# Transposed keys copied by ScalarE, six value buffers, and the sums for the output products one to a gap

## The chip, the core and the metric

The kernel runs on one core of a Trainium2 chip. The metric is the device time of one execution in microseconds. With each execution comes the core's span (about 2 us shorter: 335.8 of 337.71 us in the profile of before) and the mean clock that TensorE was granted over it, 1.0 being full speed.

## The reference

Attention over pooled keys and values, then a gated feed-forward layer, on 8 batches of 576 tokens with 8 heads of 64.

```python
k_p = k.reshape(B, H, Sp, 8, D).mean(axis=3)          # 72 pooled keys and values per head
v_p = v.reshape(B, H, Sp, 8, D).mean(axis=3)
attn = softmax(q @ k_p.T / 8)                          # cut: maximum and epsilon
x = (attn @ v_p) -> [4608 tokens, 512]
out = (np.maximum(x @ w_gate, 0.0) * (x @ w_val)) @ w_out      # 512 -> 1536 -> 512
```

## The kernel before

It is software-pipelined by hand. A loop turns over chunks of 512 tokens. Turn c runs twelve gate units of chunk c (eight 512-column matmuls each, then a relu on ScalarE and a multiplication on VectorE), the seven output products of chunk c - 1 in a scheme of the Strassen kind that needs four sums S of parts of h, and the attention of batch c + 1 (scores, exponential, value pieces with their division). GpSimd pools the keys and values of later batches meanwhile.

```python
piece_pool = ctx.enter_context(tc.tile_pool(name="piecep", bufs=4))
ps_at = ctx.enter_context(tc.tile_pool(name="ps_at", bufs=3, space=bass.MemoryType.PSUM))
...
def k_transposes(b):                       # keys of batch b, transposed in PSUM, copied out
    ps = ps_mm.tile([P, KJ + 1, KROWS], F16, name="mm_ps", tag="mm_ps")
    k_windows(b, ps, 0, KJ + 1)
    k_evacuate(b, ps, False, nc.vector)
    k_evacuate(b, ps, True, nc.vector)
...
def values(b, t):                          # one value piece: two halves, a PSUM buffer each
    x = piece_pool.tile([P, NG, 2, D], F16, name="px")
    rd = piece_pool.tile([P, 2, NG // 2, 2], F32, name="prd")
    for half in range(2):
        ps = ps_at.tile([P, 512], F32, name="at_ps", tag="at_ps")
        ...                                # four matmuls
        nc.vector.reciprocal(out=rd[:n, half], in_=pv[:, :, D:D + 2])
        nc.vector.tensor_tensor(out=x[...], in0=pv..., in1=rd..., op=ALU.mult)
...
for c in range(1, n_chunks):               # the turns
    ...
    prods, sums = out_products(c - 1)      # sums: S0 to S3, each in two halves
    ...
    others, later = attention(c + 1)       # [[keys], [], score trios ..., value pieces ...]
    for i, piece in enumerate(left):       # two pieces of batch 2, left over from turn 1
        others[1 + i].insert(0, piece)
    ...
    for i, unit in enumerate(units):
        unit()                             # a gate unit or a product
        ...
        elif i:
            run(sums[2 * i - 2:2 * i])     # two halves to a gap
        ...
        run(others[i])
```

The softmax here doesn't subtract the row's maximum and nothing guards it: scores larger than these inputs give would overflow.

Of the kernel before, what the change touches and what calls it, by code (L numbers as in the profile page):

```python
# [16 lines left out]
def kernel(  # L17
# [10 lines left out]
    nc = tc.nc  # L28

    B, H, S, D = q.shape  # L30
# [10 lines left out]
    n_chunks = NTOK // TCH  # L41
# [25 lines left out]
    relu_pool = ctx.enter_context(tc.tile_pool(name="relup", bufs=3))  # L67
    fout_pool = ctx.enter_context(tc.tile_pool(name="foutp", bufs=2))
    pexp_pool = ctx.enter_context(tc.tile_pool(name="pexpp", bufs=2))
    piece_pool = ctx.enter_context(tc.tile_pool(name="piecep", bufs=4))  # L70
    ps_mm = ctx.enter_context(tc.tile_pool(name="ps_mm", bufs=4, space=bass.MemoryType.PSUM))
    ps_at = ctx.enter_context(tc.tile_pool(name="ps_at", bufs=3, space=bass.MemoryType.PSUM))
    ps_acc = ctx.enter_context(tc.tile_pool(name="ps_acc", bufs=1, space=bass.MemoryType.PSUM))
# [43 lines left out]
    def as_rows(src, b):  # L117
        return src[b].rearrange("h (s t) d -> s h (t d)", t=POOL)
# [4 lines left out]
    def load_k(b):  # L123
        tl = kin_pool.tile([P, KJ, POOL, D], F16, name="k_in")
        k_tiles[b] = tl
        flat = k[b].rearrange("h (p j t) d -> (h p) j (t d)", p=KP, t=POOL)
        nc.gpsimd.dma_start(out=tl[:KROWS].rearrange("p j t d -> p j (t d)"), in_=flat)

    def load_v(b):
        tl = vin_pool.tile([P, H, POOL, D], F16, name="v_in")  # L130
        v_tiles[b] = tl
        nc.gpsimd.dma_start(
            out=tl[:SP].rearrange("s h t d -> s h (t d)"), in_=as_rows(v, b))
# [28 lines left out]
    def load_q(b, i0=0, n=NI):  # L162
        if b not in q16_tiles:
            q16_tiles[b] = q16_pool.tile([P, QT * D], F16, name="q16")
        cols = slice(i0 * 2 * D, (i0 + n) * 2 * D)
        flat = q[b].rearrange("h (p t) d -> (h p) (t d)", p=QP)
        nc.gpsimd.dma_start(out=q16_tiles[b][:, cols], in_=flat[:, cols])
# [22 lines left out]
    def pool_k(b, i, eng):  # L190
        src = k_tiles[b][:KROWS, 2 * i:2 * i + 2].rearrange("p j t d -> p j (t d)")
        return tree(eng, KROWS, src,
                    kps[b % 2][:KROWS, 1 + 2 * i:3 + 2 * i, :])

    def pool_v(b, g, eng):
        st = stats[b % 2][:SP, g, :].rearrange("p (x d) -> p x d", d=D)[:, 0::3, :]
        src = v_tiles[b][:SP, 2 * g:2 * g + 2].rearrange("p h t d -> p h (t d)")
        return tree(eng, SP, src, st)
# [38 lines left out]
    def run(pieces):  # L237
        for piece in pieces:
            piece()
# [7 lines left out]
    def k_windows(b, ps, w0, n):  # L247


        for w in range(w0, w0 + n):  # L250
            nc.tensor.transpose(
                out=ps[:, w, :],
                in_=kps[b % 2][:KROWS, w:w + 2, :].rearrange("p j d -> p (j d)"),
                identity=ident16[:KROWS, :KROWS])

    def k_evacuate(b, ps, upper, eng):

        ds, x, w = (slice(D, P), 1, 0) if upper else (slice(0, D), 0, 1)
        dst = kpTs[b % 2][x].rearrange("d h (s j) -> d h s j", j=KJ)[ds]
        src = ps.rearrange("d w (h s) -> d h s w", h=H)[ds, :, :, w:w + KJ]  # L260
        if eng is nc.scalar:
            eng.copy(dst, src)
        else:
            eng.tensor_copy(out=dst, in_=src)

    def k_transposes(b):
        ps = ps_mm.tile([P, KJ + 1, KROWS], F16, name="mm_ps", tag="mm_ps")
        k_windows(b, ps, 0, KJ + 1)
        k_evacuate(b, ps, False, nc.vector)
        k_evacuate(b, ps, True, nc.vector)  # L270

    qT_tiles = {}

# [14 lines left out]
    def q_dma(b):  # L288

        qT_tiles[b] = qT_pool.tile([P, NI, P], F16, name="qT")  # L290
        nc.sync.dma_start_transpose(
            out=qT_tiles[b], in_=q16_tiles[b].rearrange("p (i d) -> p i d", d=P))
# [124 lines left out]
    h_tiles = {}  # L417

    def gate_val(c, fo, t0=0, n=TCH):
        p0 = (c * TCH + t0) % RING  # L420
        cuts = [0, n] if p0 + n <= RING else [0, RING - p0, n]
        fsl = slice(fo * P, (fo + 1) * P)
        ps = []
        for w in (wg_sb, wv_sb):
            t = ps_mm.tile([P, TCH], F32, name="mm_ps", tag="mm_ps")
            for lo, hi in zip(cuts, cuts[1:]):
                x0 = (p0 + lo) % RING
                for ci in range(n_co):
                    nc.tensor.matmul(  # L429
                        out=t[:, lo:hi], lhsT=w[:, ci, fsl], rhs=x_T[:, ci, x0:x0 + hi - lo],  # L430
                        start=(ci == 0), stop=(ci == n_co - 1),
                    )
            ps.append(t)
        relu = relu_pool.tile([P, TCH], F16, name="relu")
        nc.scalar.activation(out=relu[:, :n], in_=ps[0][:, :n], func=AF.Relu)  # L435
        if c not in h_tiles:
            h_tiles[c] = h_pool.tile([P, n_fo, TCH], F16, name="h")
        nc.vector.tensor_tensor(  # L438
            out=h_tiles[c][:, fo, t0:t0 + n], in0=ps[1][:, :n], in1=relu[:, :n], op=ALU.mult)
# [48 lines left out]
    def weight_sums():  # L488

        e, f = wo_sb[:, :n_hf, :HD], wo_sb[:, :n_hf, HD:]  # L490
        g, h = wo_sb[:, n_hf:, :HD], wo_sb[:, n_hf:, HD:]
        t1, t2, t3, t4 = [wo_sums[:, i] for i in range(4)]
        return [lambda o=o, x=x, y=y, i=slice(i, i + 2): nc.vector.tensor_tensor(
                    out=o[:, i], in0=x[:, i], in1=y[:, i], op=ALU.subtract)
                for o, x, y in ((t1, f, e), (t2, h, t1), (t3, h, f), (t4, g, t2))
                for i in range(0, n_hf, 2)]
# [175 lines left out]

    gate = const_pool.tile([P, 1], F16, name="gate")

    def prep(b, load_next, behind=None):

        for i in range(KJ // 2):
            run(pool_k(b, i, nc.gpsimd))
        if behind is not None:
            nc.gpsimd.tensor_copy(out=gate, in_=behind)  # L680
        if load_next:
            load_k(b + 1)
            load_q(b + 1)
            load_v(b + 1)
        for g in range(NG):
            run(pool_v(b, g, nc.gpsimd))

# [22 lines left out]
    def weave_units(units, others):  # L710

        n, m, seq = len(others), len(units), []
        for i, unit in enumerate(units):
            seq += [unit] + others[i * n // m:(i + 1) * n // m]
        return seq

    with tc.manual_schedule():
# [110 lines left out]
             pv[0], z[10], *Sc[14:], pv[1], z[11], V[4], o[0], V[0], x[4], o[1], V[1], x[0]])  # L828
        q_dma(2)
        run([o[2], V[2], x[1], o[3], x[2], V[3], o[4]])  # L830
        prep(2, True)

        left = []
        for c in range(1, n_chunks):
            order = range(n_fo)
            if c == n_chunks - 1:

                order = [fo for i in range(n_hf) for fo in (i, n_hf + i)]
            gv = [lambda fo=fo: gate_val(c, fo) for fo in order]

            if c == 1:
                sums = weight_sums()
                units = weave_units(gv[:-1], o[5:])
            else:
                prods, sums = out_products(c - 1)
                units = []
                for fo in range(n_fo - 1):
                    units.append(gv[fo])
                    if prods and (fo not in (1, 4, 7, 10) or c == n_chunks - 1):
                        units.append(prods.pop(0))  # L850
            others = []

            prep_at = 3
            if c + 1 < B:
                others, later = attention(c + 1)
                for i, piece in enumerate(left):
                    others[1 + i].insert(0, piece)
                left = later
            if c + 2 < B:
                others[7 if c == 1 else 1].append(lambda: q_dma(c + 2))  # L860
            if c == 1:
                others[0] = [x[3]]
            for i, unit in enumerate(units):
                if i == prep_at and c + 2 < B:
                    prep(c + 2, c + 3 < B, h_tiles[c][:, 1, :1] if c > 1 else None)
                unit()
                if c == 1:
                    run(sums[i:i + 1])
                elif i:
                    run(sums[2 * i - 2:2 * i])  # L870
                if i in (0, 1) and sends:
                    sends.pop(0)()
                if i < len(others):
                    run(others[i])
                if c == n_chunks - 1:
                    if i == 14:
                        tail, last_sums = last_products(c)
                        run(last_sums[0])
                    elif i == 16:
                        run(last_sums[1])  # L880
            gv[-1]()
# [32 lines left out]
```

## Time and profile before

| | before |
|---|---|
| median of three executions | 334.46 us (334.33 to 334.75) |
| the execution that the profile shows | 337.71 us, span 335.8, mean clock 0.990 |
| TensorE busy | 325.3 us, 97% of the span |
| VectorE, ScalarE, GpSimd busy | 214.7, 128.7, 139.8 us |
| turn 2 (87.09 to 127.55 us) | 40.46 us |
| turns 3, 4, 5 | 33.79, 34.01, 33.76 us |

Read it from TensorE: it is nearly always busy, so only its holes and its clock can give anything. Both lie in turn 2.

Two readings of this trace explain words of the prediction. The trace keeps the times at which TensorE's clock changed: after its first rise it was full for 88.75 us, half for 6.83 and full for 235.52, which are 26, 2 and 69 times 3.413 us. A stretch of 3.413 us, laid end to end from the first rise, is called a clock window here. At half clock four 512-column matmuls took 1.71 us from their start to the next (96.53 to 98.24), at full clock 0.86 (90.51 to 91.37). And a "contended" sum is one made while GpSimd was at work: a pair of them took 2.31 us at 91.06, so 1.16 each, and 1.03 at 165.38 with GpSimd idle from 154.13 to 167.29.

### The profile page before, as it was taken

What the parts mean: (1) busy time and instruction counts of PE and PEld (TensorE: products, weight loads), DVE (VectorE), ACT (ScalarE), POOL (GpSimd) and SP (SyncE); (2) the same over time, 40 slices, a digit from 0 to 9 for tenths busy, and PEclk for the clock granted to TensorE, in tenths of its full rate; (3) what the DMA queues carried; (4) which work ended last, traced back from release to release, by engine and by line L of the source; (5) the groups of instructions that cost most, each with busy time, mean ns of one, the idle gap of its engine ahead of it and who ended that gap; (6) DMA issues with size and microseconds to landing.
All of it is one profiled execution on the core that took longest, in us unless ns stands there. A gap on an engine that the chain in (4) does not pass through costs nothing.

```text
span 335.8 us, 6528 instructions
## 1 busy us (share of the span) xinstructions
PE 325.3 (97%) x2526; PEld 214.2 (64%) x2526; DVE 214.7 (64%) x456; ACT 128.7 (38%) x295; POOL 139.8 (42%) x186
## 2 busy tenths in 40 slices
PE   8899999999969999999999999999999999999995
PEld 2578875455536665766898966655666556566574
DVE  7465637768666757785777667766576464464562
ACT  1544562473426224722471247124822332232231
POOL 8557419999999801993099309300000000000000
PEclk9999999999969999999999999999999999999999
DMA  7999998998559246963984462243022300300224
GB/s 112 190 204 201 200 214 159 188 153 171 106 101 185 47 90 94 205 101 74 159 158 79 81 107 58 33 64 104 1 24 56 113 5 0 98 29 3 65 75 110
DMA packets 51006, 35.41 MB, mean 105 GB/s; under 512 B 30432, under 2 KB 45024, under 8 KB 50976
## 3 DMA queue, kind: packets, MB, share of 16 engines
q0 software_dynamic: 18304, 18.88, 34.3%
q1 hardware_dynamic: 32528, 16.00, 24.0%
q8 instruction: 19, 0.31, 0.4%
q10 hardware_dynamic: 144, 0.13, 0.1%
q14 instruction: 11, 0.09, 0.1%
HBM read 37.75 MB, written 9.44 MB: 141 GB/s over the span
## 4 chain that ended last, share of the span: by engine, by line
PE 90%; DVE 5%; DMA 2%; ACT 1%; issue 1%; POOL 1%; DVEq 0%; ACTq 0%; POOLq 0%
PE mm_ps L429 54%; PE acc_ps L521 19%; PE at_ps L310 5%; PE mm_ps L467 3%; PE at_ps L388 3%; PE mm_ps L594 2%; DMA q<-in_q_dram 2%; DVE px L394 1%; DVE h L438 1%; PE mm_ps L411 1%; DVE sum L512 1%; PE mm_ps L281 1%; PE mm_ps L341 1%; PE mm_ps L365 1%; ACT pexp L370 1%
## 5 line engine op out<-in xcount | busy, mean ns | idle before, releaser
L438 DVE TENSOR_TENSOR h<-mm_ps,relu 128x512 f16<-128x512 f32 (+1 forms) x120 | 76.4, 637 | 87.6 <-PE mm_ps L429 79.8
L435 ACT ACTIVATE relu<-mm_ps 128x512 f16<-128x512 f32 (+1 forms) x120 | 66.5, 554 | 137.4 <-PE mm_ps L429 135.3
L429 PE MATMUL mm_ps<-x_T,wv_sb 128*128 128x512 f16 (+1 forms) x528 | 114.0, 342 | 0.1
L429 PE MATMUL mm_ps<-x_T,wg_sb 128*128 128x512 f16 (+1 forms) x528 | 114.0, 342 | 0.0
L429 PEld LDWEIGHTS <-wv_sb 128*128 128x128 f16 x528 | 51.7, 98 | 42.9 <-issue 1.1
L429 PEld LDWEIGHTS <-wg_sb 128*128 128x128 f16 x528 | 48.7, 98 | 28.9 <-issue 1.4
L324 ACT ACTIVATE expT<-at_ps 72x288 f16<-72x288 f32 (+2 forms) x128 | 39.1, 374 | 19.0 <-PE at_ps L310 18.9
L521 PEld LDWEIGHTS <-sum 128*128 128x128 f16 x336 | 32.1, 98 | 7.2
L394 DVE TENSOR_TENSOR px<-at_ps,prd 128x256 f16<-128x256 f32 (+1 forms) x80 | 33.8, 423 | 2.7
L181 POOL TENSOR_TENSOR tree_b<-tree_a 72x256 f32<-72x256 f32 (+1 forms) x42 | 32.0, 763 | 3.3
L521 PE MATMUL acc_ps<-wo_sums,sum 128*128 128x256 f16 x252 | 31.0, 272 | 0.0
L175 POOL TENSOR_TENSOR tree_a<-v_in 72x512 f32<-72x512 f16 x24 | 29.9, 1244 | 0.1
L521 PEld LDWEIGHTS <-h 128*128 128x128 f16 x252 | 23.9, 99 | 4.1
L175 POOL TENSOR_TENSOR tree_a<-k_in 96x512 f32<-96x512 f16 x18 | 20.7, 1149 | 11.5 <-DMA k_in<-in_k_dram 11.5
L521 PE MATMUL acc_ps<-wo_sb,h 128*128 128x256 f16 x168 | 21.1, 276 | 0.0
L529 DVE TENSOR_TENSOR rows<-acc_ps,mid 128x512 f32<-128x512 f32 x21 | 14.5, 689 | 8.8 <-PE acc_ps L521 8.8
L680 POOL COPY gate<-h 128x1 f16<-128x1 f16 x4 | 1.9, 463 | 43.4 <-DVE h L438 43.4
L512 DVE TENSOR_TENSOR sum<-h 128x768 f16<-128x768 f16 x28 | 19.8, 746 | 0.1
L388 PEld LDWEIGHTS <-expT 72*128 72x128 f16 (+1 forms) x280 | 13.0, 100 | 7.5 <-DVE px L394 1.6
L393 DVE RECIPROCAL prd<-at_ps 128x4 f32<-128x4 f32 (+1 forms) x80 | 13.7, 172 | 4.0 <-PE at_ps L388 3.9
L388 PE MATMUL at_ps<-stat,expT 72*128 72x65 f16 (+1 forms) x280 | 14.8, 194 | 1.4 <-DVE px L394 1.4
L186 POOL TENSOR_TENSOR stat<-tree_b 72x128 f16<-72x128 f32 x24 | 12.1, 506 | 1.9
(106 smaller groups left out, 300.2 us busy)
## 6 DMA issues: line engine op xcount, KB each, us to landing
out_dram<-rows SPq DMA_DIRECT2D x24, 256.0 KB
k_in<-in_k_dram POOLq DMA_DIRECT2D x7, 576.0 KB, 8.0
q<-in_q_dram POOLq DMA_DIRECT2D x7, 576.0 KB, 9.9
v_in<-in_v_dram POOLq DMA_DIRECT2D x6, 576.0 KB, 13.5
wg_sb<-in_moe_w_gate_dram POOLq DMA_DIRECT2D x6, 256.0 KB, 10.9
wv_sb<-in_moe_w_val_dram POOLq DMA_DIRECT2D x6, 256.0 KB, 10.8
wo_sb<-in_moe_w_out_dram POOLq DMA_DIRECT2D x3, 512.0 KB, 9.6
v_in<-in_v_dram POOLq DMA_DIRECT2D x2, 512.0 KB, 11.3
```

The source lines that it names most:

```text
L175: eng.tensor_tensor(out=cell["a"][:n], in0=src[:, :, :4 * D], in1=src[:, :, 4 * D:], op=ALU.add)
L181: eng.tensor_tensor(out=cell["c"][:n], in0=a[:n, :, :2 * D], in1=a[:n, :, 2 * D:], op=ALU.add)
L310: nc.tensor.matmul(out=ps[:SP, c0:c0 + cnt * QP], lhsT=kpTs[b % 2][j][:, h, :], rhs=queries(b, h, i0, cnt), start=True, stop=True,)
L324: nc.scalar.activation(out=out_ap, in_=in_ap, func=AF.Exp, scale=EXP_SCALE)
L388: nc.tensor.matmul(out=ps[:n, c0:c0 + D + 1], lhsT=weights(b, h, t), rhs=stats[b % 2][:SP, g, s0:s0 + D + 1], start=True, stop=True,)
L394: nc.vector.tensor_tensor(out=x[:n, half * NG // 2:(half + 1) * NG // 2, :, :], in0=pv.rearrange("p g (x c) -> p g x c", x=2)[:, :, :, :D] ...
L429: nc.tensor.matmul(out=t[:, lo:hi], lhsT=w[:, ci, fsl], rhs=x_T[:, ci, x0:x0 + hi - lo], start=(ci == 0), stop=(ci == n_co - 1),)
L435: nc.scalar.activation(out=relu[:, :n], in_=ps[0][:, :n], func=AF.Relu)
L438: nc.vector.tensor_tensor(out=h_tiles[c][:, fo, t0:t0 + n], in0=ps[1][:, :n], in1=relu[:, :n], op=ALU.mult)
L512: nc.vector.tensor_tensor(out=S[k][:, i], in0=x[:, i], in1=y[:, i], op=op)
L521: nc.tensor.matmul(out=ps[:, tb, :], lhsT=lhs[:, i, tb * P:(tb + 1) * P], rhs=rhs[:, i, :], start=(first and tb == 0 and i == 0), stop=(tb ...
L529: nc.vector.tensor_tensor(out=out_ap, in0=x, in1=y, op=ALU.add)
```

## The change

Its intent is to take VectorE's queue off TensorE's path at the start of a turn. Three parts are named in its title; the fourth (score trios, that is the scores in threes, of turn 2 moved one unit back, in the hunk on `left`) is not. `prep` is also split in two functions, but both are called at the same place in the same order, so nothing follows from it and that part is cut here.

```diff
-    piece_pool = ctx.enter_context(tc.tile_pool(name="piecep", bufs=4))
+    piece_pool = ctx.enter_context(tc.tile_pool(name="piecep", bufs=6))
...
-        k_evacuate(b, ps, False, nc.vector)
-        k_evacuate(b, ps, True, nc.vector)
+        k_evacuate(b, ps, False, (nc.scalar if b > 2 else nc.vector))
+        k_evacuate(b, ps, True, (nc.scalar if b > 2 else nc.vector))
...
+        SUMS_AT = [1, 2, 3, 4, 5, 6, 13, 14]
...
-                for i, piece in enumerate(left):
-                    others[1 + i].insert(0, piece)
+                if left:
+                    others[1:2] = [[piece] for piece in left]
...
-                elif i:
-                    run(sums[2 * i - 2:2 * i])
+                elif c == n_chunks - 1:
+                    run(sums[max(2 * i - 2, 0):2 * i])
+                elif i in SUMS_AT:
+                    sums[SUMS_AT.index(i)]()
```

More of the change, by code (lines that the diff above doesn't have):

```diff
@@ L673, with prep_k @@
     gate = const_pool.tile([P, 1], F16, name="gate")
-    def prep(b, load_next, behind=None):
+    def prep_k(b, load_next, behind=None):
         for i in range(KJ // 2):
@@ L684, in prep, with prep_v @@
             load_v(b + 1)
+    def prep_v(b):
         for g in range(NG):
@@ L830 @@
         run([o[2], V[2], x[1], o[3], x[2], V[3], o[4]])
-        prep(2, True)
+        prep_k(2, True)
+        prep_v(2)
+        SUMS_AT = [1, 2, 3, 4, 5, 6, 13, 14]
         left = []
@@ L851 @@
             others = []
-            prep_at = 3
+            prep_v_at = 3
             if c + 1 < B:
                 others, later = attention(c + 1)
-                for i, piece in enumerate(left):
-                    others[1 + i].insert(0, piece)
+                if left:
+                    others[1:2] = [[piece] for piece in left]
                 left = later
@@ L863 @@
             for i, unit in enumerate(units):
-                if i == prep_at and c + 2 < B:
-                    prep(c + 2, c + 3 < B, h_tiles[c][:, 1, :1] if c > 1 else None)
+                if i == 3 and c + 2 < B:
+                    prep_k(c + 2, c + 3 < B, h_tiles[c][:, 1, :1] if c > 1 else None)
+                if i == prep_v_at and c + 2 < B:
+                    prep_v(c + 2)
                 unit()
```

## The prediction

> **What bounds the kernel now.** I read the page first: its busy shares, then the slices. TensorE is busy 325.3 of 335.8 us, no other engine over 64%, and the chain that ended last is 90% TensorE. So the time is the length of TensorE's stream, plus its holes, plus any time at a lowered clock. In the slices (one digit is 8.4 us) only one place away from the two ends shows both:
>
> ```profile
> PE   8899999999969999999999999999999999999995
> ...
> DVE  7465637768666757785777667766576464464562
> ...
> PEclk9999999999969999999999999999999999999999
> ```
>
> The twelfth digit, 92 to 101 us, is a 6 in the row of TensorE and a 6 in the row of its clock. The source says what lies there: the loop turns over 512-token chunks, and its turn c = 2 begins at about 87.1 us (the transposes of batch 3's pooled keys end its first unit). I cut the busy time at the turns' starts, which the chain and TensorE's timeline give (turns 2, 3 and 5):
>
> ```profile
> 87.09:127.55 40.46, 37.79 (x268) 22.83 (x267) 27.84 (x55) 13.74 (x30) 28.05 (x36) 0.92 0.52 103
> 127.55:161.34 33.79, 33.79 (x254) 21.26 (x252) 24.04 (x47) 13.52 (x30) 19.13 (x25) 1.00 0.67 120
> ...
> 195.35:229.11 33.76, 33.76 (x252) 21.18 (x251) 23.59 (x47) 13.52 (x30) 11.03 (x13) 1.00 0.41 66
> ```
>
> Columns: window, length, then busy time of PE, PEld, DVE, ACT, POOL, then clock, DMA share, GB/s. Turns 3 and 5 take 33.8 us with TensorE never idle. Turn 2 takes 40.46. It does more work by only two value pieces of batch 2 left over from turn 1, 16 small matmuls each of which the timeline places in 0.25 to 0.26 us, so it should take 33.8 + 0.5 = 34.3. **The loss there is 40.46 - 34.3 = 6.15 us**, and no other turn has one. Two-microsecond windows show its form:
>
> ```profile
> 92.00:94.00 2.00, 0.65 (x6) 0.20 (x4) 1.93 (x5) 0.17 (x1) 1.89 (x3) 1.00 0.00 0
> 94.00:96.00 2.00, 1.03 (x7) 0.66 (x8) 1.97 (x6) 0.52 (x2) 1.84 (x3) 0.72 0.09 18
> 96.00:98.00 2.00, 1.66 (x5) 0.69 (x5) 1.73 (x5) 0.70 (x2) 2.00 (x5) 0.50 0.73 138
> 98.00:100.00 2.00, 2.00 (x7) 0.67 (x5) 0.00 (x0) 0.60 (x1) 1.91 (x3) 0.50 1.10 188
> 100.00:102.00 2.00, 2.00 (x14) 1.57 (x13) 1.74 (x3) 1.00 (x3) 1.92 (x3) 0.57 1.14 213
> ```
>
> First a hole with VectorE (third busy figure) full, then half clock. The clock was at half for 1.12 us of the second row ((1 - 0.72)/0.5 x 2), all of the next two and 1.72 of the last: 6.84 us. Matmuls of 512 columns then take twice as long, so about 5.5 us of work at half clock cost 2.7 us; the holes cost the other 3.4. The timelines of TensorE and of VectorE name the cause:
>
> ```profile
> 92.33 0.32 PE L388 MATMUL at_ps<-stat,expT 72*64 72x65 f16 x4
> 94.09 0.32 PE L388 MATMUL at_ps<-stat,expT 72*64 72x65 f16 x4 [1.45 <-DVE px L394]
> 94.64 0.31 PE L310 MATMUL at_ps<-qT,kpT1l 128*72 128x288 f16 x1 [0.23 <-DVE px L394]
> ```
> ```profile
> 89.53 0.74 DVE L264 COPY kpT1l<-mm_ps 64x576 f16<-64x576 f16 x1
> 90.28 0.76 DVE L264 COPY kpT1u<-mm_ps 64x576 f16<-64x576 f16 x1
> 91.06 2.31 DVE L512 TENSOR_TENSOR sum<-h 128x768 f16<-128x768 f16 x2
> 93.39 0.18 DVE L393 RECIPROCAL prd<-at_ps 128x4 f32<-128x4 f32 x1
> 93.61 0.42 DVE L394 TENSOR_TENSOR px<-at_ps,prd 128x256 f16<-128x256 f32 x1
> ```
>
> Three PSUM buffers of the attention pool serve the value pieces and the scores. Two pieces need four. The fourth half waits for VectorE to read the first, and VectorE has 0.74 + 0.76 us of key copies and 2.31 us of sums queued ahead of that read. Turns 3 to 7 have the same VectorE queue, but no value piece beside it, so there it stays beside TensorE's work.
>
> [...] the window that dropped it (91.47 to 94.88, counting back from the drop) was not idle: from the timeline and widths TensorE worked about 30% of it. Near 13 to 16 us, between the first transposes, a window filled to about 56% did not drop it. [...] a pair of these sums takes 2.31 us while GpSimd is in its key tree (88 to 96 us), and 1.03 at 165.38 while GpSimd is idle. [...]
>
> **The change part by part.** *Key copies to ScalarE.* Ten copies (five batches, two each) leave VectorE, 5 x 1.50 = 7.5 us. On ScalarE a 16-bit copy from PSUM took 585 ns at 512 columns and 1012 at 1024, so 0.834 ns a column and 0.64 us at 576. Two take 1.25 us, in a hole of ScalarE: before its copy of the first product it idles 1.9 us in each turn. That copy comes out at about the same time (in turn 4 at about 164.7 us, as now), and the next user of its bank is 4 us off. Worth nothing in turns 3 to 6, part of the loss in turn 2.
>
> *Sums one to a gap.* The eight additions remain. The order listing puts the first after the first product, the second after the next gate unit, and the last two around the sixth product. In turn 2 only one stands before each value piece.
>
> *The left-over pieces.* The listing also shows a move that the few words do not name: in turn 2 piece one is followed by a gate unit before piece two, and every score trio comes one unit later. TensorE has 1.73 us of other work while VectorE empties the first piece.
>
> *Six buffers.* In the trace before no division waits for a transfer, so two more are worth 0.
>
> Working turn 2 by hand with the trace's durations: VectorE ends its product at 89.6; first sum (1.16, contended) to 90.8; piece one to 91.9. TensorE runs gate unit two to 92.24, piece two at once (its second half needs the buffer freed at about 91.4), and gate unit three to 94.2. VectorE: product of unit two 92.5 to 93.1, second sum to between 93.6 and 94.2, both halves of piece two 1.2 us more, the first freed after 0.65. The trio on TensorE from 94.2 needs these two buffers, wants the last at 94.5 and gets it between 94.9 and 95.4: **a new hole of 0.4 to 1.0, say 0.8 us**. A clock window holding all of it is still 70% busy, so no drop.
>
> At the end of turn 2 the third product needs the bank read out and the last sum. Gate unit nine ends at about 114.0, piece five follows. VectorE then has product 0.65, sum 0.55 to 1.1, piece five 1.1, read-out 0.65, last sum 0.55: done at about 118.0 to 118.5, where TensorE wants its second half at 117.7. **Say 0.5 us.** In turns 3 and 4 piece five is not in that stretch and GpSimd's trees end about as the sum starts (154.1 and 187.7 us): 0. The last turn keeps its order.
>
> Sum: 6.15 - 0.8 - 0.5 = 4.85; 334.46 - 4.85 = 329.6 us.
>
> **The rivals.** *The clock falls anyway*, because the 0.8 us hole joins others. For it: an idle window is not needed, 30% busy sufficed. Against it: 56% did not. It would cost about 2.7 more: 332.3. *VectorE's queue simply moves*, the last sums holding up the last product in turns 2 to 5. For it: two buffer reads and a contended sum in one gap. Against it: VectorE is idle about 10 us of each turn, and the sum has over 3 us. At 0.4 us in each it makes 330.8. *No hole is left*: if sums run at 0.55 us, all 6.15 return, 328.3. *ScalarE becomes late with the keys*: the first scores come 5 us after the transposes in turn 2 and 3 us after them in the others, against 1.4 us of copies, so I give it little.
>
> **Range and chances.** The floor is 328.3, since turn 2's loss is all there is to remove. A gain over 2% needs 6.7 us, more than that loss, so it has 0.03. Both new holes at their worst give about 330.5; a part of a clock drop would pass that. Range 328.4 to 331.2. Slower by over 2% would need a new throttle in several turns: 0.02.
>
> **What would show it.** Turn 2 at 35 to 36 us, the others at 33.8; clock full from 92 to 102; no wait over 0.3 us for the division ahead of a value piece; a wait below 1 us of the second and third score of turn 2; the key copies on ScalarE near 0.64 us; a wait at the seventh product of turn 2 alone. I am wrong if the clock still halves in turn 2, or if any of turns 3 to 7 grows by more than 0.3 us.

## The result and the profile after

The changed kernel took 332.37 us (median of six, 332.12 to 333.23), before 334.78 in the same rounds (six, 334.33 to 336.16). The ratio is 0.9925, 95% interval 0.9903 to 0.9946: 2.8 us slower than predicted, outside the range of 328.4 to 331.2. Ratios here are the mean time of one kernel's fast runs over that of the other's fast runs of the same rounds, so not quite the ratio of the medians.

Yet the changed kernel's profile shows nearly everything that was predicted. First the page's slices, to be held against the same two rows of before: the 6 in both is gone.

```profile
PE   8899999999999999999999999999999999999995
...
PEclk9999999999999999999999999999999999999999
```

Next the busy times cut at its turns 2, 3 and 5 (window, length, then PE, PEld, DVE, ACT, POOL, clock, DMA share, GB/s):

```profile
87.12:122.09 34.97, 34.92 (x268) 21.59 (x267) 24.40 (x53) 14.81 (x32) 28.88 (x37) 1.00 0.63 120
122.09:155.88 33.79, 33.79 (x254) 21.26 (x252) 22.58 (x45) 14.80 (x32) 19.71 (x25) 1.00 1.08 122
...
189.89:223.65 33.76, 33.76 (x252) 21.19 (x251) 20.91 (x45) 14.80 (x32) 10.91 (x13) 1.00 0.39 67
```

Turn 2 went from 40.46 to 34.97 us with the clock at 1.00; the other turns did not move. The timeline of VectorE in turn 2 shows why; one sum and no key copy is left ahead of the first value piece:

```profile
88.95 0.69 DVE L438 TENSOR_TENSOR h<-mm_ps,relu 128x512 f16<-128x512 f32 x1 [1.04 <-PE mm_ps L429]
89.56 1.34 DVE L512 TENSOR_TENSOR sum<-h 128x768 f16<-128x768 f16 x1
90.83 0.17 DVE L393 RECIPROCAL prd<-at_ps 128x4 f32<-128x4 f32 x1
...
93.15 0.55 DVE L512 TENSOR_TENSOR sum<-h 128x768 f16<-128x768 f16 x1
```

TensorE's timeline has no marked idle time at the second piece or at the scores after it. (Idle time above 0.15 us is marked in brackets at the end of a line: how long the engine stood still before the instruction, and what released it.)

```profile
92.36 0.44 PE L388 MATMUL at_ps<-stat,expT 72*64 72x65 f16 x8
...
94.83 0.31 PE L310 MATMUL at_ps<-qT,kpT1l 128*72 128x288 f16 x1
```

And the key copies on ScalarE (group view; partitions x elements, count, then busy us and mean ns of one, idle before) take what was estimated:

```profile
L262 ACT COPY kpT1u<-mm_ps 64x576 f16<-64x576 f16 x3 | 1.9, 635 | 0.1
L262 ACT COPY kpT1l<-mm_ps 64x576 f16<-64x576 f16 x3 | 1.9, 632 | 1.7 <-PE mm_ps L251 1.7
```

So the two profiles differ by 335.8 - 330.4 = 5.4 us of span, and the medians by 2.4 us. The 3.0 us between these two figures are the puzzle. The profiled execution of after took 332.44 us, like its fellows. The profiled execution of before took 337.71, which is 3.25 over the median that was given with it.

### The profile page after: what moved, and what is told of

Its sections match the earlier page's. It is cut to its first block, busy times and chain, and to the rows that moved or that the text cites. A ratio compares the mean times of both kernels' runs of the same rounds, so it can differ in the third digit from the quotient of the medians.

```text
span 330.4 us, 6528 instructions
## 1 busy us (share of the span) xinstructions
PE 322.4 (98%) x2526; PEld 212.9 (64%) x2526; DVE 204.9 (62%) x446; ACT 135.0 (41%) x305; POOL 140.2 (42%) x186
## 4 chain that ended last, share of the span: by engine, by line
PE 94%; DVE 2%; DMA 2%; issue 1%; POOL 1%; ACT 0%; DVEq 0%; POOLq 0%
PE mm_ps L429 56%; PE acc_ps L521 20%; PE at_ps L310 4%; PE mm_ps L467 3%; PE at_ps L388 3%; PE mm_ps L594 2%; DMA q<-in_q_dram 2%; DVE px L394 1%; PE mm_ps L365 1%; PE mm_ps L411 1%; PE mm_ps L281 1%; PE mm_ps L341 1%; PE mm_ps L251 1%; PE mm_ps L245 0%; POOL k_in L147 0%
## 5 line engine op out<-in xcount | busy, mean ns | idle before, releaser
L394 DVE TENSOR_TENSOR px<-at_ps,prd 128x256 f16<-128x256 f32 (+1 forms) x80 | 33.8, 423 | 2.7
L181 POOL TENSOR_TENSOR tree_b<-tree_a 72x256 f32<-72x256 f32 (+1 forms) x42 | 33.4, 796 | 3.3
L175 POOL TENSOR_TENSOR tree_a<-v_in 72x512 f32<-72x512 f16 x24 | 28.7, 1197 | 0.1
L175 POOL TENSOR_TENSOR tree_a<-k_in 96x512 f32<-96x512 f16 x18 | 21.6, 1201 | 14.2 <-DMA k_in<-in_k_dram 14.2
L512 DVE TENSOR_TENSOR sum<-h 128x768 f16<-128x768 f16 x28 | 17.4, 628 | 0.0
```

Source lines behind the costliest of these rows:

```text
L175: eng.tensor_tensor(out=cell["a"][:n], in0=src[:, :, :4 * D], in1=src[:, :, 4 * D:], op=ALU.add)
L181: eng.tensor_tensor(out=cell["c"][:n], in0=a[:n, :, :2 * D], in1=a[:n, :, 2 * D:], op=ALU.add)
L394: nc.vector.tensor_tensor(out=x[:n, half * NG // 2:(half + 1) * NG // 2, :, :], in0=pv.rearrange("p g (x c) -> p g x c", x=2)[:, :, :, :D] ...
L512: nc.vector.tensor_tensor(out=S[k][:, i], in0=x[:, i], in1=y[:, i], op=op)
```

## The experiments

**Theory A.** TensorE's clock falls in turn 2 only in some executions of before, when one clock window happens to catch most of the holes; the profile was taken in such an execution, the median was not. **Rival B.** The clock falls in every execution of before, and the profiled one was longer for another reason. Every experiment ran six times (one of them profiled), except the two looks.

### The kernel before again: b_again

No edit.

> The kernel before, unchanged. Theory A (the clock falls only in some executions): the executions split into those with a mean clock near 0.990 and a span near 335.8 us, like the profiled one, and those with a clock of 0.997 or more and a span near 332.5 to 333.2, that is 2.7 us less; the median stays near 334.5 us and so most belong to the second kind. Theory B (the clock falls in turn 2 of every execution, and the profiled one was longer for another reason): every execution has a clock of 0.988 to 0.991.

The lists of executions that came with this and the later runs give span and clock of 51 executions of the kernel before, on four chips:

| mean clock | executions | span, mean | spans |
|---|---|---|---|
| 0.997 or more | 22 | 332.46 us | 331.7 to 333.2 |
| 0.994 or 0.995 | 28 | 334.30 us | 333.4 to 335.4 |
| 0.990 | 1 | 336.7 us | |
| the profile of before, 0.990 | (1) | 335.8 us | |

The classes answer to no, one or two clock windows at half speed. A window of 3.41 us (half of the 6.83 us that the first profile spent at half clock) loses 1.7 us of work by this estimate, which makes a mean clock of 0.995 over 334.3 us, and the first two classes are 1.84 apart. B falls: 22 of 51 executions never lost the clock. The other half of theory A, that the holes are what drops it, is tested further below. Two things were expected wrongly. Most executions do not keep the clock; on this chip 12 of 18 lost it. And those that lose it mostly lose one window (0.995), not the two of the first profile (0.990). The times of the first two classes do not overlap (333.47 to 335.09 and 335.28 to 337.20 us), so the three executions around 334.46 us on the first chip, whose clocks are not listed, belong to the first class (mean time 334.31 us); of the six in the result's rounds, 335.49 and 336.16 belong to the second.

The profile of this run is of an execution that kept its clock (0.999). Turn 2 in it, and two stretches of it:

```profile
87.66:124.43 36.77, 35.07 (x268) 21.82 (x267) 26.86 (x55) 13.74 (x30) 28.52 (x37) 1.00 0.61 117
```
```profile
92.00:94.00 2.00, 1.52 (x13) 0.65 (x11) 1.90 (x6) 0.60 (x1) 1.97 (x2) 1.00 0.00 0
94.00:96.00 2.00, 0.78 (x6) 0.51 (x6) 2.00 (x5) 0.81 (x2) 1.87 (x3) 1.00 0.30 60
```

The holes are there (PE busy 1.52 and 0.78 of 2 us), the clock is not lowered, and the turn takes 36.77 us, not 40.46. The hole at the second piece is also shorter than in the first profile, 0.48 us of marked idle time against 1.45, because the pair of sums ahead of it took 1.34 us, not 2.31. So three things made up the 6.15 us of the prediction, and two of them vary by execution: the clock, and how long the sums run beside GpSimd.

### One part at a time on the kernel before

**keys_only**: the two `k_evacuate` lines of the diff alone.

```diff
-        k_evacuate(b, ps, False, nc.vector)
+        k_evacuate(b, ps, False, (nc.scalar if b > 2 else nc.vector))      # and the upper half
```

> The kernel before with only the key copies of batches 3 to 7 on ScalarE. 1.5 us leaves VectorE ahead of the first value piece of turn 2. Under theory A the holes of turn 2 (3.4 us in the profile) shrink by about 1.5 and the time falls to about 333.0 us, ratio 0.9955. Under B the clock still falls in part of the executions and they save 1.5 to 4.2. Turns 3 to 7 unchanged at 33.8 us; copies on ScalarE 0.64 us each.

Median 333.27 us, ratio 0.9921 (0.9887 to 0.9956), all six at a clock of 0.997 or more, mean span 331.48. The key copies alone give 0.98 us against undisturbed executions of before (1.17 against the six of the same chip), less than the 1.5 expected, and keep the clock.

**sums_only**: `SUMS_AT` and the lines that use it alone.

```diff
-                elif i:
-                    run(sums[2 * i - 2:2 * i])
+                elif i in SUMS_AT:                     # last turn kept as it was
+                    sums[SUMS_AT.index(i)]()
```

> The kernel before with only the sums one to a gap. One contended sum of 1.16 us leaves the queue ahead of the first piece and one sum of 0.6 to 1.0 the queue ahead of the second. Under theory A holes shrink by 1.5 to 2, to about 332.9 us, ratio 0.995. If the late sums hold up the seventh product, as a rival of the prediction had it, turn 2 to 5 grow by up to 0.4 us each and the gain is gone.

Median 334.89 us, ratio 0.9961 (0.9921 to 1.0002). Three executions kept the clock (331.80 mean) and three were at 0.995 (333.93). The rival that late sums hold up the seventh product fell: in the profile turns 3 to 5 took 33.79, 34.00 and 33.77 us. The waits of the second and third score remain here, 0.49 us of marked idle time each, and the profiled execution is one that lost its clock. Windows of two microseconds:

```profile
92.00:94.00 2.00, 0.96 (x11) 0.56 (x11) 1.93 (x6) 0.41 (x1) 1.92 (x3) 1.00 0.00 0
94.00:96.00 2.00, 1.51 (x6) 0.70 (x6) 1.52 (x5) 0.81 (x2) 1.84 (x4) 0.72 0.53 102
96.00:98.00 2.00, 2.00 (x6) 0.79 (x5) 0.00 (x0) 0.60 (x1) 1.84 (x4) 0.50 1.17 216
```

The busy figure of the first row is less than half, and the clock falls in the second.

**pieces_only**: the hunk on `left` alone.

```diff
-                for i, piece in enumerate(left):
-                    others[1 + i].insert(0, piece)
+                if left:
+                    others[1:2] = [[piece] for piece in left]
```

> The kernel before with only the moved score trios of turn 2 (a gate unit between the second value piece and the scores). The wait of the second piece's second half (1.6 us) stays, the three waits of the scores (1.8 us) go: about 332.9 us, ratio 0.995, under theory A. The hole of 1.6 us alone leaves a window more than half busy, so no execution should have a clock below 0.995.

Median 335.10 us, ratio 0.9992 (0.9947 to 1.0036): a miss. In the profile turn 2 is shorter (35.8 us, from the keys' transposes to those of the next turn), but turn 3 has a new hole: a division on VectorE waited 4.0 us for a transposing transfer that still read its value buffer, and TensorE waited 1.8 us for VectorE at the seventh product. One execution of six was at 0.995. This was the first sign that the number of value buffers matters.

### The buffers: undo_bufs, pieces_bufs, bufs_only

**undo_bufs** is the changed kernel with four buffers, **pieces_bufs** is pieces_only with six, **bufs_only** is the kernel before with six.

```diff
-    piece_pool = ctx.enter_context(tc.tile_pool(name="piecep", bufs=6))
+    piece_pool = ctx.enter_context(tc.tile_pool(name="piecep", bufs=4))    # undo_bufs
```

> The changed kernel with four value buffers in place of six. The prediction said six are worth nothing: spans 330.2 to 331.3 us as the changed kernel has. The rival that the run of the moved pieces alone raised (a division in turn 3 waited 4.0 us for a transposing transfer that still read its buffer, and TensorE 1.8 us for it): that wait appears again, spans of 331.5 to 333 us in all or most executions.

Median 335.16 us, ratio 0.9964 (0.9915 to 1.0014). Three executions at full clock (mean span 331.70), three at 0.995 (335.03). The profile is of one of the latter, and its clock fell at 155.03 us, in turn 3 and not in turn 2. In its list of waits (who waited for whom: total us, times, longest) and on TensorE's timeline, in turn 3:

```profile
DVE px L394 <- DMA x_T<-px: 4.2, 1, 4.2
...
PE acc_ps L521 <- DVE rows L529: 2.5, 1, 2.5
```
```profile
151.07 1.03 PE L429 MATMUL mm_ps<-x_T,wv_sb 128*128 128x512 f16 x4
154.56 1.72 PE L521 MATMUL acc_ps<-wo_sb,sum 128*128 128x256 f16 x8 [2.47 <-DVE rows L529]
```

With six buffers this wait did not show in any of the twelve executions of the changed kernel by its times. The prediction's "two more are worth 0" is refuted.

> The kernel before with the moved score trios and six value buffers. If the wait for the transfer ate the gain of the trios when they moved alone, it is gone here: no wait of VectorE for a transfer of the transposed values, turn 3 back at 33.8 us, undisturbed spans near 331.6 us (332.7 less the 1.0 that turn 2 gained). If buffers are worth nothing, spans stay at 332.2 to 333.0 with the wait of 4 us still there.

Median 333.48 us, ratio 0.9941 (0.9901 to 0.9981), all six at full clock, mean span 332.17, four of them at 331.5 to 331.7 as expected. The wait for the transfer is gone. Two executions had 333.0 and 333.6; the first of them is the profiled one, and in it the pair of sums took 2.17 us and the second piece's wait was long again.

> The kernel before with six value buffers and nothing else. Tells where the executions of before at 0.995 (11 of 18 on this chip) lost their clock. Theory A1 (in turn 2, where the holes are): still about half at 0.995 with spans of 333.7 to 335.1, the others at 332.0 to 333.2. Theory A2 (in turn 3, where a division waits for a transfer when there are four buffers): none or nearly none at 0.995, all at 332.0 to 333.2.

Median 335.66 us, ratio 1.0015 (0.9977 to 1.0053). Three at full clock (332.77), two at 0.995 and one at 0.987. In the profile the clock fell at 94.98 us. So A1: before lost its clock in turn 2, not at the buffers. The buffers matter only once the other parts have shortened turn 2. That turn 3 then meets its transfers at a busier time is what the DMA share suggests (148 to 152 us: 1.31 in undo_bufs, 0.47 in the profile of before, which was 4 to 5 us behind there; 0.27 at 152 to 156); no run tested it.

### Is it the holes that drop the clock? long_hole, fill, fill_bufs, fill_all and two looks

**long_hole** makes the first sum of turn 2 twice on the kernel before.

```diff
                     run(sums[2 * i - 2:2 * i])
+                    if c == 2 and i == 1:
+                        run(sums[0:2])
```

> The kernel before with the first sum of turn 2 made twice (same values), which puts 1.3 to 2.3 us more on VectorE ahead of the first value piece. Theory A: holes of 3.7 to 5.5 us, so nearly every window position holds one that is less than half busy: all executions at 0.995 or 0.99, none at 0.997 or more, spans of 335.5 to 338. Rival (the drop has nothing to do with the holes): the split of before, and spans 1.3 to 2.3 us above before in each kind.

Median 338.92 us, ratio 1.0081 (1.0045 to 1.0116). All six lost the clock: two at 0.995, four at 0.990 (before: 1 of 51), mean span 336.9. The hole in its profile, on TensorE's timeline:

```profile
96.13 0.31 PE L388 MATMUL at_ps<-stat,expT 72*64 72x65 f16 x4 [2.89 <-DVE px L394]
```

**fill** puts eight matmuls that nothing reads into the wait of the second piece, on the kernel before; **fill_bufs** is the same with six buffers.

```diff
-    def values(b, t):
+    def values(b, t, fill=0):
         ...
         for half in range(2):
+            if half and fill:
+                warm(fill)               # fill = 8 for the second piece of turn 2
```

> The kernel before with eight idle matmuls (1.73 us of TensorE work that nothing reads) ahead of the second half of the second value piece of turn 2, where TensorE waits. Theory A (the clock falls when one 3.4 us window catches most of the holes, which depends on where the windows stand): every execution has a clock of 0.997 or more, and spans of 333.2 to 333.8 us, that is the undisturbed 332.7 of before plus 1.1 at most for matmuls that outlast the wait; in spite of the added work the mean is not above that of before. Rival (the clock falls for another reason): as many executions at 0.995 as in before, and spans above 334.5.

Median 335.24 us, ratio 1.0012 (0.9961 to 1.0063). Four executions kept the clock, mean span 333.32; two were at 0.995 with 336.5 and 336.8. A miss of theory A as stated, so I supposed that these two lost their clock at the buffers of turn 3.

> The kernel before with the eight idle matmuls of the earlier run and six value buffers. Two of six executions of that run were at 0.995 against theory A. Theory A3 (those two lost their clock in turn 3, at the wait of a division for a transfer that four buffers allow, and turn 2 was cured): none below 0.997 here, spans of 333.0 to 333.6 us. Rival (filling the wait in turn 2 does not keep the clock): one to three of six at 0.995 again.

Median 334.64 us, ratio 1.0022 (0.9974 to 1.0071). Two of six lost the clock again (0.995 and 0.990), so A3 falls.

**fill_look1**, **fill_look2**: two looks at fill_bufs for the profile of such an execution. **fill_all**: fill_bufs with three more idle matmuls ahead of each of the two scores that wait.

```diff
+        if b == 3 and (h, j) in ((0, 1), (1, 0)):
+            warm(3)
         for c0, i0, cnt in parts:
```

> A look at the kernel with eight idle matmuls and six buffers, for the profile of an execution that lost its clock (one in three did). If it does: theory A wants a window under half busy in turn 2 just before the drop, behind long sums; the rival wants the drop elsewhere or after a full window. If it keeps its clock, the look tells nothing.

> The same look again, for the same reason and with the same expectation.

The first look kept its clock (span 334.5). The second lost it (336.4, clock 0.992). VectorE's and TensorE's timelines and the windows of that second look:

```profile
91.53 2.34 DVE L514 TENSOR_TENSOR sum<-h 128x768 f16<-128x768 f16 x2
...
95.60 1.63 DVE L514 TENSOR_TENSOR sum<-sum,h 128x768 f16<-128x768 f16 x2
```
```profile
97.82 0.31 PE L310 MATMUL at_ps<-qT,kpT1l 128*72 128x288 f16 x1 [1.59 <-DVE px L396]
```
```profile
96.00:98.00 2.00, 0.41 (x4) 0.21 (x4) 1.93 (x6) 0.41 (x1) 1.92 (x5) 1.00 0.54 103
98.00:100.00 2.00, 2.00 (x9) 0.85 (x8) 0.31 (x1) 1.00 (x2) 1.98 (x3) 0.77 1.11 200
```

Both pairs of sums ran long, the third score then waited 1.59 us for VectorE after the filled place, and the clock fell at about 99.1 us, right after.

> The kernel before with six value buffers, the eight idle matmuls, and three more ahead of each of the second and the third score of turn 2, so that TensorE is above 80% busy in every clock window there. Theory A (a window less than about half busy drops the clock): none of six below 0.997, spans of 333 to 333.8. If one or more is at 0.995 or 0.99 again, how busy TensorE is in turn 2 does not decide the drop alone, and its condition stays open.

None of the six lost its clock. Mean span 333.15, median 334.95 us, ratio 1.0001 (0.9963 to 1.0038): fourteen idle matmuls, 14 x 0.216 = 3.0 us of TensorE's time for nothing (a gate unit's eight 512-column matmuls took 1.73 us in this profile, 85.39 to 87.12), cost nothing that six executions can show on the mean (the interval is 1.3 us to either side), since they took the place of waits and kept the clock. Six executions are few (before lost the clock in 4 of 11 on this chip, so six in a row would keep it by luck about once in fifteen times), but with the windows below theory A stands, with a correction: all waits of the turn count, not the one at the second piece alone.

How empty must a window be? The packed traces keep the times at which the clock changed. In each trace the stretches at full clock are whole numbers of 3.413 us (88.75 us is 26 of them, 324.27 us in after is 95, 327.68 us is 96), and five traces have a single window of 3413 ns at half clock. So the windows can be laid from the first rise of the clock, also where it never fell. That rise stands at 3.99 to 6.98 us in the twenty traces: the windows lie differently in every execution. `prof LABEL --windows` then gives TensorE's busy time in each. It counts the whole record of each matmul, and these overlap (before, 90.51 us: four of 512 columns stand as 1.03 us, and the next four begin 0.86 us later), so it is more than the work done (the prediction's 30% and 56% were estimated from widths: by this measure they are 1.73 and 3.05 us of 3.41). The emptiest windows of all traces after the first 12 us are these:

| window, us | run | TensorE busy, us of 3.41 | the clock after it |
|---|---|---|---|
| 94.05 to 97.46 | long_hole | 0.63 | fell |
| 151.61 to 155.03 | undo_bufs | 0.95 | fell |
| 95.66 to 99.07 | fill_look2 | 1.54 | fell |
| 91.47 to 94.88 | before | 1.73 | fell |
| 91.46 to 94.87 | sums_only | 1.88 | fell |
| 91.57 to 94.98 | bufs_only | 2.04 | fell |
| 152.12 to 155.53 | pieces_only | 2.04 | held |
| 91.44 to 94.85 | pieces_bufs | 2.10 | held |
| 96.29 to 99.70 | fill_look1 | 2.12 | held |
| 92.74 to 96.15 | keys_only | 2.14 | held |
| 93.65 to 97.06 | b_again | 2.15 | held |

Of these windows, every one below 2.04 us was followed by a fall of the clock and every one above was not; of the two at 2.04 one was. Only just after the first rise did the clock hold after a window of 1.99 us too (keys_only, 7.41 to 10.82), so the edge is not exact by this measure. The longest marked wait in the window ahead of the fall was 1.45 us in the first profile of before and 0.49 us in bufs_only. The pair bufs_only and b_again shows best what theory A means: the holes of turn 2 are the same (marked 0.47, 0.24, 0.49, 0.49 and 0.48, 0.23, 0.49, 0.49 us), but a window of bufs_only caught the first three and the start of the fourth, one of b_again only the last three, and only bufs_only lost its clock.

### One part undone from the changed kernel, and a step further

**a_again** is the changed kernel unchanged, on another chip.

> The changed kernel on the chip of the other runs. Theory A: no hole in turn 2 over 0.2 us and six value buffers, so no execution below a clock of 0.997, spans of 330.2 to 331.3 us as on the first chip, and 2.0 to 2.4 us under the undisturbed executions of before (332.0 to 333.2). If the first chip was merely quieter, some executions here are at 0.995.

Median 332.79 us, ratio 0.9925 (0.9896 to 0.9955); all six at 0.998 or more, spans 330.2 to 331.2. With the first six, twelve of twelve kept the clock, mean span 330.62.

**undo_keys**: both `k_evacuate` calls back to `nc.vector`. **undo_sums**: back to `run(sums[2 * i - 2:2 * i])`. **undo_pieces**: back to `others[1 + i].insert(0, piece)`. Each is one hunk of the diff above, reversed:

```diff
-        k_evacuate(b, ps, False, (nc.scalar if b > 2 else nc.vector))      # undo_keys
+        k_evacuate(b, ps, False, nc.vector)
-                elif i in SUMS_AT:                                         # undo_sums
-                    sums[SUMS_AT.index(i)]()
+                elif i:
+                    run(sums[2 * i - 2:2 * i])
-                    others[1:2] = [[piece] for piece in left]              # undo_pieces
+                    others[1 + i].insert(0, piece)
```

> The changed kernel with the key copies back on VectorE. 1.5 us returns ahead of the first value piece of turn 2; TensorE has 1.73 us of gate unit beside it, so a hole of 0.6 to 1.3 us comes back at the second piece: spans of 331.0 to 331.9, clock 0.997 or more in all.

Median 333.52 us, ratio 0.9949 (0.9918 to 0.9980), all at full clock, mean span 331.38. The span is as expected, the hole is not: the profiled execution (the shortest, 330.9) has no marked wait at the second piece, but 0.17 and 0.23 us at the second and third score.

> The changed kernel with the sums in pairs as before. A second sum (0.6 to 1.2 us) ahead of the first value piece, and a pair (1.3 to 2.0) ahead of the second: holes of 0.2 to 1.1 at the second piece and 0.5 to 1.3 at the scores, spans of 331.0 to 332.3, clock 0.997 or more in nearly all.

Median 333.42 us, ratio 0.9945 (0.9907 to 0.9984). Five at full clock, mean span 331.46; the sixth, slow (336.9, clock 0.992), is not compared. In the profile the pair of sums ran 2.35 us, and the score waited 1.1 us.

> The changed kernel with the score trios of turn 2 where they were, straight after the second value piece. No wait at the second piece (one sum and no key copy ahead of the first), but the second and the third score each wait about 0.65 us for the exponential of the one before: spans of 331.3 to 332.2 us, clock 0.997 or more in all.

Median 333.55 us, ratio 0.9945 (0.9922 to 0.9968), all at full clock, mean span 331.37. The second and third score each waited 0.49 us of marked idle time for the exponential of the one before.

So each of the three parts is worth about 0.8 us when taken from the whole (331.38, 331.46 and 331.37 against 330.62), and the four together 1.84 us against undisturbed executions of before. The fourth part, the buffers, is worth 1.08 by the three executions of undo_bufs at full clock (331.70). These four add to 3.4 us, nearly twice 1.84, so the parts are not additive: what one is worth depends on which others are there.

**keys_from_2** goes a step further: keys of batch 2, in turn 1, on ScalarE too.

```diff
-        k_evacuate(b, ps, False, (nc.scalar if b > 2 else nc.vector))
+        k_evacuate(b, ps, False, (nc.scalar if b > 1 else nc.vector))      # and the upper half
```

> The changed kernel with the key copies of batch 2, in turn 1, on ScalarE as well. In turn 1 TensorE stood for 0.3 to 0.8 us near 64.6 us behind VectorE's key copies and weight sums; this goes, spans of 329.6 to 330.6 us, 0.3 to 0.6 under the changed kernel. If the wait there comes from the weight sums alone, spans stay at 330.2 to 331.2.

Median 332.69 us, ratio 0.9919 (0.9897 to 0.9941), mean span 330.55 against 330.62. The wait near 64.6 us is gone from its profile, but the gain is within the scatter. It cannot be called better than the changed kernel.

## Why the prediction was wrong

*What bounds the kernel, and the cause.* Right. TensorE's stream with a hole and a lowered clock in turn 2, made by VectorE's queue ahead of the value pieces. The changed profile has neither.

*"The loss there is 40.46 - 34.3 = 6.15 us", and from it "334.46 - 4.85".* **This is the step that failed.** The 6.15 us are a true reading of the one profiled execution, which took 337.71 us, but they were taken off the median of executions that took 334.46. Executions with full clock have a mean span of 332.46, so 335.8 - 332.46 = 3.3 us of those 6.15 were not in them: the clock had not fallen there, and the sums could run shorter. What the median could give was 6.15 - 3.3 = 2.8 us before new holes (turn 2 of b_again gives 36.77 - 34.3 = 2.5 directly). The result file said so beforehand: the profiled execution was 3.25 us over the median, and nothing was made of it. "The floor is 328.3" fell with the same step.

*The new holes, "0.8" and "0.5".* Right in place, too large. At the scores TensorE started the third at 94.83 us where the second's matmuls would have let it start at about 94.7, because the second sum took 0.55 us, the best case of the range. At the end of turn 2 the gate unit ahead of the seventh product and that product took 3.40 us on TensorE's timeline (115.08 to 118.48), 0.36 more than their 1.73 + 1.31. Together 0.5 us, not 1.3. With both corrections the prediction would have been 334.46 - 2.8 + 0.5 = 332.2; measured were 332.37.

*Key copies on ScalarE.* Right: 0.63 us each, in a hole of ScalarE, no delay of TensorE, nothing gained in turns 3 to 6.

*Sums one to a gap.* The eight additions stayed whole, only their places changed.

*"Six buffers worth 0".* Wrong for the changed kernel, right for the kernel before. The trace before could not show a wait that arises only when turn 2 is shorter. The changed kernel had all parts, so this did not move the number.

*The rivals.* "The clock falls anyway" did not happen, in twelve of twelve; that its 332.3 us is nearly the measured 332.37 is chance. "The queue simply moves" did not either: turns 3 and 5 are 33.79 and 33.76 us as before. The rival that was missing is that the clock does not fall in the executions that are timed.

*What would show it.* Turn 2 "at 35 to 36 us" was 34.97, the others stayed at 33.8, the clock stayed full, the key copies were near 0.64 us. All signs named were met and the time was still missed, since none of them asked whether the profile of before was like the timed executions.

What stays open: what decides the length of the sums in one execution. The same pair took 1.33 or 1.34 us in b_again, pieces_only, fill and bufs_only, and 2.17 to 2.35 in before, keys_only, pieces_bufs, undo_sums and fill_look2. That GpSimd is behind it is an estimate from the 1.03 us of such a pair beside an idle GpSimd; no run took GpSimd's work away, and in b_again, where the pair took 1.34, GpSimd was busy for 1.97 of the 2 us from 92.00. Open too is the exact fill of a window after which the clock falls.

## What to carry to other kernels

Before a loss is read off a profile and subtracted from a measured median, compare the profiled execution's own time and mean clock with the others: what only it has cannot be gained. The holes of a busy TensorE cost twice when one clock window caught enough of them (the clock fell after windows with TensorE busy for 0.63 to 2.04 of 3.41 us), so executions split into classes, and the change that removed the holes also removed the slower classes: 1.84 us within the full-clock class and 2.9 us on the mean of all (333.55 us of span for the 51 executions of before against 330.62). When one wait is taken away, look for the buffers that the old wait was protecting.
